# One core, forward and backward of an adaLN block: where the scalings of a gradient's rows run, one product more ahead of a norm gradient's ScalarE steps, and two index operations behind transposed rows

## The chip, the cores and the metric

The kernel runs on one core of one Trainium2 chip. The metric is the device time of one execution in microseconds (us). Below, PE is TensorE, PEld its weight loads, DVE is VectorE, ACT is ScalarE, POOL is GpSimd, SP is SyncE; SPq and ACTq are the instruction queues of SP and ACT, from which they issue DMAs. L548 is line 548 of the kernel before.

## The reference

A forward pass and its vector-Jacobian product. With `mod = silu(c) @ w_mod` cut into six rows of 1024 (sa, ca, ga, sb, cb, gb):

```python
h = layernorm(x) * (1 + ca) + sa
x = x + ga * irfft2(rfft2(h) * (w_r + 1j * w_i))        # S = 2048 tokens, D = 1024
h = layernorm(x) * (1 + cb) + sb
x = x + gb * (gelu(layernorm(h) @ w1 + b1) @ w2 + b2)   # F = 3584
```

The outputs are x and the gradients of A_x, w_r, w_i, w1, b1, w2, b2, c and w_mod for a given `grad_out` of 2048 x 1024. Two of them matter here. The gradient of w_mod is an outer product: for each of the six rows r, `out_9[:, r] = u * gmod[r]`, with u = silu(c) (1024 values) and gmod[r] the gradient of that row of mod (1024 values). The gradient of w1 (`out_4`, 1024 x 3584) is the product of the normalized tokens with the gradient of the MLP's inner layer, summed over 2048 tokens.

## The kernel before, in words

All large products run on PE in bf16 into PSUM tiles of 128 x 512 f32, and everything else is arranged around an order of PE's instructions that is written out by hand. A framework assigns semaphores and buffers, and orders each engine's instructions by priority and by its own estimate of times; `tc.issue_after(x)` ties an instruction to a place behind x on an engine, and `behind(a, b)` makes a follow b in that order without a semaphore. PSUM has three groups of tiles: "s" and "d" with two buffers each, and "f" with four.

**The start.** `grad_out` comes in four blocks of 512 tokens (`gos[0..3]`, loaded by SP from L355, in order with blocks of w_mod, transposed pieces of w2 and the tokens x). `turn_go(j, cch)` (L554) transposes 128 columns of block j: four small products with the identity (L559) into one PSUM tile, from group "s" for even cch and "d" for odd; DVE (even cch, L563) or ACT (odd cch, L566) scales that tile into `gBoT[j]`. The eight turns of block 0 stand alone. The turns of block j+1 are threaded between the 16 products `pp` of block j (L584: two tiles of eight products, each product n reads column block n of `gBoT[j]` and a transposed piece of w2); `TURN_AT` says ahead of which product each turn stands. `pp` takes tiles of group "f", and its results are cast to bf16 on DVE or ACT (L540). Beside this, index tables for the sine and cosine matrices are built: POOL makes products of row and column numbers (L382), and one DVE operation masks them (L413, `trig_idx`). Five of these tables are wanted at the start; the last two go into `gidx2`. Much later (from 57 us) ACT takes sines of them. Behind the start come the remaining products of grad_out with w2 (L548, from 42 us), layer norms of x on DVE and ACT, and folds of the tokens on DVE.

**The last norm gradient.** Near the end the backward inverse transform gives four blocks of tokens; `consume_bwd` (L1580) takes block i through the gradient of the first layer norm: DVE multiplies and sums rows (`scaled_rows`, L1374, giving `s1c`), then four times `ln_bwd` (L1361): one DVE sum (L1365), one ACT operation that needs it and `s1c` (L1368), one DVE addition. To keep PE busy meanwhile, `fill(n)` calls a generator, `pieces()` (L1689), that emits n further pieces of other work. At this place a piece is one tile of out_4: 16 products (L1770, `gw1acc`, a tile of group "f"), a cast on ACT (L1774, `gwo`) and a store. The tuples in `consume_bwd` say how many pieces are emitted at each place. The ACT steps of `ln_bwd` are tied behind the cast of the piece that was emitted last (`w1g["ev"]`).

**The end.** `gw1_quads` (L1654) makes the last two column blocks of out_4 by Strassen-like sums: for each of four column groups c it has seven products of eight matmuls (`gqy`, `gqx`, `gqw`, L1686), ACT copies of intermediate tiles (L1668, `snap`), casts on ACT (L1676) and additions on DVE (L195) that make the results. Through the last pieces, two chains of work on w_mod's gradient run on other engines:

- `gmod_chain` (L1273): for rows 4, 2, 1, 0, eight steps each: load a block of w_mod, multiply and sum with gmod[r] on DVE (L1287, into `gu`). From `gu` come the gradient of c, a small vector (`gc_bf`, L1876), its transpose on PE (L210, `ptr`) and its store.
- `gmod_scaled` (L1293): for the same rows, eight steps each: `gw = gmod[r] * u` for 128 rows of out_9 (128 x 1024 bf16, L1298 on ACT), and its store of 256 KB (L1299, issued by POOL). `gw` goes round five buffers (in the tile `otl`), so scaling n needs the store of scaling n-5 to have landed.

The last loop (L1858) emits, for each of the `left` remaining pieces, the piece, some steps of the chain and one or two steps of the scaling:

```python
        for _ in range(2 if n >= left - 9 else 1):
            next(scaled, None)
```

Of the kernel before, what the change touches and what calls it, by code (L numbers as in the profile page):

```python
# [17 lines left out]
P = 128  # L18
# [17 lines left out]
def kernel(  # L36
# [366 lines left out]
    gslots.update({6 + k: (gidx[:, 1, :], gidx3)[k // 2][:, k % 2 * 512:(k % 2 + 1) * 512] for k in range(4)})  # L403
    trig_in = [None]

    def trig_idx(slot, colv, rowv, nrow, width, modn, cosine):
# [5 lines left out]
        n = nrow * width  # L412
        nc.vector.tensor_scalar(out=idx[:, 0:n], in0=idx[:, 0:n], scalar1=modn - 1, scalar2=None, op0=ALU.bitwise_and)  # L413
        return idx[:, 0:n].rearrange("p (r w) -> p r w", w=width), modn
# [129 lines left out]
    def ph_part(fc, js):  # L544
        for j in js:
# [4 lines left out]
            ph_out(fc, j, pp)  # L550

    turn_in = [None, None]

# [56 lines left out]
    def gen_rows():  # L610
# [7 lines left out]
        return em1  # L618

    def behind(ins, later):  # L620
        tc.add_manual_dep(ins.ins, later.ins.name, mybir.DependencyInfo(mybir.DependencyClass.NoSync, mybir.DependencyReason.DATA),
                          reason="order")

# [669 lines left out]
    def gmod_scaled(rows):  # L1293
        for n in range(len(rows) * NDC):
            k, jc = n // NDC, n % NDC
            gw, r = w1g["gw"][n % 5], rows[k]
            with tc.issue_after(w1g["ev"].ins):
                nc.scalar.activation(out=gw, in_=w1g["gr"][k], func=ACT.Identity, scale=u_rt[:, jc:jc + 1])  # L1298
            nc.gpsimd.dma_start(out=out_9[jc * P:(jc + 1) * P, r * D:(r + 1) * D], in_=gw)  # L1299
            yield  # L1300
# [283 lines left out]
    def consume_bwd(i, o4, tmp, tmp2, n1, eb):  # L1584
# [197 lines left out]
    def fill(n):  # L1782
        for _ in range(n):
            next(todo)
        done[0] += n
# [124 lines left out]
```

## Time and profile before

| | us |
|---|---|
| median of 3 runs | 1373.33 |
| range of these runs | 1371.58 to 1376.87 |
| profiled execution, its own time | 1372.29 |
| span of the profiled execution, first to last instruction | 1370.3 |
| PE busy | 1345.6 (98% of the span) |
| DVE busy | 1077.2 (79%) |
| ACT busy | 792.4 (58%) |
| POOL busy | 390.3 (28%) |

How to read the rows below: a row of the timeline gives the start, the duration and the engine of an instruction (or of xN that follow each other), its line, its operation, out<-in, and in square brackets how long the engine stood idle before it and what ended this. Matmuls are pipelined, so a run of N of them reads a little longer than the distance to the next row. A row of waits gives "engine tile line <- releaser: total us, times, longest us". A row of windows gives the busy us of each engine in a stretch, with the number of instructions, then the granted TensorE clock (1.00 is full), the busy share of the DMA engines and the GB/s.

### The profile page before, as it was taken

The page shows a single profiled execution, that of the slowest core. Times are in us where ns is not written, and L with a number is a line of the kernel's source. Part 1 is how long each engine was busy: PE and PEld are TensorE (multiplying, and loading weights), DVE is VectorE, ACT ScalarE, POOL GpSimd, SP SyncE. Part 2 cuts the span into 40 slices and gives each one's busy share as a digit, 9 for nine tenths or more (in the row PEclk, how much of TensorE's full clock was granted, in tenths as well). Part 3 has the DMA queues.
Part 4 walks back from the last instruction along what each step waited for, and adds up shares of the span by engine and source line. Part 5 has one row for each costly group of instructions (what it writes and reads, how often), then busy time and mean ns, then how long its engine had stood idle before and what let it go on. Part 6 is the DMA issues. An engine that isn't in the chain of part 4 may idle for free. (4 is left out here: it accounts for less than half of the span.)

```text
span 1370.3 us, 18631 instructions
## 1 busy us (share of the span) xinstructions
PE 1345.6 (98%) x6899; PEld 651.0 (48%) x6899; DVE 1077.2 (79%) x1467; ACT 792.4 (58%) x1120; POOL 390.3 (28%) x436
## 2 busy tenths in 40 slices
PE   7999999999999999999999999999999999999997
PEld 4445566444444444444444444444644555444443
DVE  6997889999988878787620578889888488976985
ACT  4864667767877765665414593445732554544456
POOL 6273642411112122212211010112344330332163
PEclk9999999999999999999999999999999999999999
DMA  9975594899787887698999699988579878899876
GB/s 326 322 196 140 160 256 154 250 279 318 262 254 252 212 261 246 199 289 233 284 278 224 181 217 311 296 254 257 179 238 270 222 160 237 207 245 251 201 271 244
DMA packets 356401, 330.08 MB, mean 241 GB/s; under 512 B 203866, under 2 KB 298736, under 8 KB 356182
## 3 DMA queue, kind: packets, MB, share of 16 engines
q1 hardware_dynamic: 314310, 201.02, 57.2%
q0 software_dynamic: 35232, 120.00, 26.0%
q10 hardware_dynamic: 6768, 7.87, 1.7%
q8 instruction: 54, 0.88, 0.3%
q14 instruction: 37, 0.30, 0.1%
HBM read 165.73 MB, written 114.87 MB: 205 GB/s over the span
## 5 line engine op out<-in xcount | busy, mean ns | idle before, releaser
L1230 PE MATMUL pg<-w1T,gzr 128*128 128x512 bf16 x896 | 195.8, 380 | 0.0
L548 PE MATMUL pp<-gBoT,wt 128*128 128x512 bf16 x832 | 185.4, 379 | 3.2 <-ACT pho L540 1.9
L1076 PEld LDWEIGHTS <-w 128*128 128x128 bf16 x896 | 87.2, 98 | 107.4 <-issue 2.9
L1230 PEld LDWEIGHTS <-gzr 128*128 128x128 bf16 x896 | 86.5, 98 | 108.5 <-issue 5.8
L548 PEld LDWEIGHTS <-wt 128*128 128x128 bf16 x832 | 81.0, 98 | 97.9 <-issue 5.3
L1770 PE MATMUL gw1acc<-gzh,n3n 128*128 128x512 bf16 x512 | 111.8, 380 | 0.0
L1076 PE MATMUL pz<-n3Ta,w 128*128 128x512 bf16 x448 | 98.8, 380 | 1.4 <-ACT gt L1079 1.4
L1076 PE MATMUL pz<-n3Tb,w 128*128 128x512 bf16 x448 | 99.0, 380 | 0.0
L1770 PEld LDWEIGHTS <-n3n 128*128 128x128 bf16 x640 | 62.3, 98 | 76.7 <-issue 3.1
L195 DVE TENSOR_TENSOR ct<-ct 128x2048 bf16<-128x2048 bf16 (+1 forms) x84 | 91.5, 1120 | 4.3 <-ACT n L514 2.0
L1079 ACT ACTIVATE gt<-pz,b_col 128x512 bf16<-128x512 f32 x112 | 72.8, 682 | 37.3 <-PE pz L1076 33.1
L1130 PEld LDWEIGHTS <-hhA 128*128 128x128 bf16 x608 | 58.9, 98 | 73.2 <-issue 3.0
L1087 ACT ACTIVATE gt<-gt 128x2048 bf16<-128x2048 bf16 x28 | 53.5, 1911 | 58.3 <-DVE gt L195 58.3
L1411 PE MATMUL gw2acc<-gB,hhsA 128*128 128x512 bf16 x384 | 84.8, 380 | 0.0
L195 DVE TENSOR_TENSOR gt<-gt,gt 128x2048 bf16<-128x2048 bf16 x56 | 68.4, 1223 | 17.7 <-ACT gt L1089 16.8
L1419 ACT CAST gwo<-gw2acc 128x512 bf16<-128x512 f32 x40 | 23.5, 588 | 87.5 <-PE gw2acc L1411 84.2
L1411 PEld LDWEIGHTS <-hhsA 128*128 128x128 bf16 x384 | 37.5, 98 | 43.5
L1083 ACT ACTIVATE gt<-gt 128x2048 bf16<-128x2048 bf16 x28 | 53.4, 1908 | 3.1 <-DVE hhC L195 2.4
L540 ACT CAST pho<-pp 128x512 bf16<-128x512 f32 x68 | 38.6, 584 | 27.3 <-PE pp L548 24.1
L1774 ACT CAST gwo<-gw1acc 128x512 bf16<-128x512 f32 x40 | 23.0, 579 | 53.6 <-PE gw1acc L1770 41.6
L1089 ACT ACTIVATE gt<-gt 128x2048 bf16<-128x2048 bf16 x28 | 53.3, 1905 | 0.3
L1411 PE MATMUL gw2acc<-gB,otl 128*128 128x512 bf16 x224 | 50.0, 380 | 0.0
(414 smaller groups left out, 2710.3 us busy)
## 6 DMA issues: line engine op xcount, KB each, us to landing
gzr<-d_gz SPq DMA_DIRECT2D x28, 512.0 KB
d_ph<-pho POOLq DMA_DIRECT2D x21, 512.0 KB, 5.5
wblk<-in_w_mod_dram SPq DMA_DIRECT2D x10, 1024.0 KB
out_dram<-otl POOLq DMA_DIRECT2D x40, 256.0 KB, 4.1
d_hh<-hhA POOLq DMA_DIRECT2D x19, 512.0 KB, 5.6
wrw<-in_w_mod_dram SPq DMA_DIRECT2D x32, 256.0 KB
w<-in_B_w_dram SPq DMA_DIRECT2D x7, 1024.0 KB
hhC<-d_ph SPq DMA_DIRECT2D x14, 512.0 KB
```

The lines of the kernel that those rows point to most:

```text
L195: return nc.vector.tensor_tensor(out=out, in0=a, in1=b, op=op)
L540: copy(out=ov, in_=pv)
L548: last_pe[0] = nc.tensor.matmul(pp[:], lhsT=wt[:, fc % 4, cch, :], rhs=gBoT[j][:, cch, :], start=(cch == 0), stop=(cch == NDC - 1))
L1076: last_pe[0] = nc.tensor.matmul(pz[:], lhsT=w1s[g][:, cch, k * P:(k + 1) * P], rhs=n3T[:, cch, :], start=(cch == 0), stop=(cch == NDC - 1))
L1079: z_in = nc.scalar.activation(out=zb[:, k, :], in_=pz[:], func=ACT.Identity, bias=b1_col[:, fc:fc + 1], scale=1.0)
L1083: nc.scalar.activation(out=av, in_=zb, func=ACT.Square)
L1087: nc.scalar.activation(out=sg, in_=bv, func=ACT.Sigmoid, scale=2.0 * GK)
L1089: nc.scalar.activation(out=bv, in_=bv, func=ACT.Sigmoid, scale=-2.0 * GK)
L1130: last_pe[0] = nc.tensor.matmul(pbs[i][:], lhsT=hh[:, k, i * P:(i + 1) * P], rhs=wp[:, k, :], start=False, stop=(g == 6 and k == 3))
L1230: last_pg[0] = nc.tensor.matmul(pgs[i][:], lhsT=gzs[b, g][:, k, i * P:(i + 1) * P], rhs=w1Ts[g][:, k, h * KH:(h + 1) * KH], start=(g == 0 ...
L1411: nc.tensor.matmul(acc[:], lhsT=hh_of(fc)[:, t, :], rhs=gBs[t // 4][:, t % 4, h * KH:(h + 1) * KH], start=(t == 0), stop=(t == NT - 1))
L1770: nc.tensor.matmul(acc[:], lhsT=n3ns[t // 4][:, t % 4, cch * P:(cch + 1) * P], rhs=gz2[t // 8][:, t % 8, :], start=(t == 0), stop=(t == NT ...
```

## The change

It has three parts.

1. In the start, the DVE masks of the last two index tables (`idx_in[-2]`, `idx_in[-1]`) are ordered behind the DVE halves of turns 2 and 4 of block 1. `behind` moves up in the file, without a change in it. POOL's part of the tables stays where it is.
2. In `consume_bwd`, block 3 has nine pieces instead of eight ahead of `scaled_rows`, and one instead of two behind it. PE's own order of instructions is the same, word for word.
3. In `gmod_scaled`, rows 4, 2 and 1 are scaled on ACT as before, but their stores are issued by ACT; row 0 is scaled on DVE, with its stores on POOL. The last loop takes two scalings per piece for the first eight pieces, none with the ninth, one per piece for the next eight, and two per piece for the last five (rows 4 and 2, then row 1, then row 0).

```diff
-        nc.vector.tensor_scalar(out=idx[:, 0:n], in0=idx[:, 0:n], scalar1=modn - 1, scalar2=None, op0=ALU.bitwise_and)
+        idx_in.append(nc.vector.tensor_scalar(out=idx[:, 0:n], in0=idx[:, 0:n], scalar1=modn - 1, scalar2=None, op0=ALU.bitwise_and))
...
     first_idx.update({k: token_idx(k) for k in (4, 2, 3)})
+    idx_late = {2: idx_in[-2], 4: idx_in[-1]}
...
                     turn_go(j + 1, TURN_AT.index(n))
+                    if j == 0 and TURN_AT.index(n) in idx_late:
+                        behind(idx_late[TURN_AT.index(n)], turn_in[0])
...
-            with tc.issue_after(w1g["ev"].ins):
-                nc.scalar.activation(out=gw, in_=w1g["gr"][k], func=ACT.Identity, scale=u_rt[:, jc:jc + 1])
-            nc.gpsimd.dma_start(out=out_9[jc * P:(jc + 1) * P, r * D:(r + 1) * D], in_=gw)
+            if k < 3:
+                with tc.issue_after(w1g["ev"].ins):
+                    nc.scalar.activation(out=gw, in_=w1g["gr"][k], func=ACT.Identity, scale=u_rt[:, jc:jc + 1])
+            else:
+                with tc.issue_after(w1g["dve"].ins):
+                    w1g["dve"] = nc.vector.tensor_scalar(out=gw, in0=w1g["gr"][k], scalar1=u_rt[:, jc:jc + 1], scalar2=None,
+                                                         op0=ALU.mult)
+            (nc.scalar if k < 3 else nc.gpsimd).dma_start(out=out_9[jc * P:(jc + 1) * P, r * D:(r + 1) * D], in_=gw)
...
-        fill((0, 6, 6, 8)[i])
+        fill((0, 6, 6, 9)[i])
...
-        fill((4, 1, 2, 2)[i])
+        fill((4, 1, 2, 1)[i])
...
-        for _ in range(2 if n >= left - 9 else 1):
+        for _ in range(2 if n < 8 else 1 if 8 < n < 17 else 2 if n >= left - 5 else 0):
             next(scaled, None)
```

How the order of the instructions changes on DVE and ACT, at the three places that the prediction speaks of. The lines of the changed kernel are a few higher than those of the kernel before (L563 there is L567 here, L1298 is L1302, L1368 is L1376, L1774 is L1782).

DVE at the start, before: `gidx_269` is the tile of the last two index tables, `gBoT_133` and `gBoT_134` are the turned blocks 0 and 1, `gb_col` the column they are scaled with.

```order
L523 COPY gb_col<-pc 128x8
L563 TENSOR_SCALAR gBoT_133,gu<-pt,gb_col 128x512 x4
L413 TENSOR_SCALAR gidx_269<-gidx_269 128x1024
L563 TENSOR_SCALAR gBoT_134,gu<-pt,gb_col 128x512
L413 TENSOR_SCALAR gidx_269<-gidx_269 128x1024
L563 TENSOR_SCALAR gBoT_134,gu<-pt,gb_col 128x512 x3
```

The same place after:

```order
L523 COPY gb_col<-pc 128x8
L567 TENSOR_SCALAR gBoT_133,gu<-pt,gb_col 128x512 x4
L567 TENSOR_SCALAR gBoT_134,gu<-pt,gb_col 128x512 x2
L413 TENSOR_SCALAR gidx_269<-gidx_269 128x1024
L567 TENSOR_SCALAR gBoT_134,gu<-pt,gb_col 128x512
L413 TENSOR_SCALAR gidx_269<-gidx_269 128x1024
L567 TENSOR_SCALAR gBoT_134,gu<-pt,gb_col 128x512
```

The two masks have moved behind the first two turned tiles of block 1. As a consequence of the new order the framework has also re-sorted some casts between DVE and ACT up to about 90 us: ahead of the last mask of a 128 x 512 table in `smax`, DVE has 16 casts from PSUM tiles of 512 columns where it had 19.

ACT from the last norm gradient to the first scalings, before: `ct<-xt,s1c,sc` is the ACT step of `ln_bwd`, `gwo_9683<-gw1acc` the cast of a piece, `otl<-gr,u_rt` a scaling, `accCA` and `accSA` are column sums.

```order
L1774 CAST gwo_9683<-gw1acc 128x512 x7
L1368 ACTIVATE ct<-xt,s1c,sc 128x1024 x3
L1774 CAST gwo_9683<-gw1acc 128x512
L1368 ACTIVATE ct<-xt,s1c,sc 128x1024
L1774 CAST gwo_9683<-gw1acc 128x512
L233 COPY ct<-accCA 64x512
L1774 CAST gwo_9683<-gw1acc 128x512 x2
L1850 ACTIVATE sr<-accSA_10559 1x512
L1850 ACTIVATE sr<-accSA_10560 1x512
L1774 CAST gwo_9683<-gw1acc 128x512
L1298 ACTIVATE otl<-gr,u_rt 128x1024
L1774 CAST gwo_9683<-gw1acc 128x512
```

The same place after:

```order
L1782 CAST gwo_9683<-gw1acc 128x512 x8
L1376 ACTIVATE ct<-xt,s1c,sc 128x1024 x3
L1782 CAST gwo_9683<-gw1acc 128x512
L1376 ACTIVATE ct<-xt,s1c,sc 128x1024
L233 COPY ct<-accCA 64x512
L1782 CAST gwo_9683<-gw1acc 128x512 x2
L1858 ACTIVATE sr<-accSA_10559 1x512
L1858 ACTIVATE sr<-accSA_10560 1x512
L1782 CAST gwo_9683<-gw1acc 128x512
L1302 ACTIVATE otl<-gr,u_rt 128x1024 x2
L1307 DMA out_dram<-otl 128x1024 x2
L1782 CAST gwo_9683<-gw1acc 128x512
```

One cast has moved from behind the fourth `ln_bwd` step to ahead of the first. Two scalings and two DMA issues now stand where one scaling stood.

DVE at the end, before: `wrw,gu<-wrw,gr` is a step of the chain, `t_11132<-gu` and `gc_bf` lead to the gradient of c, `gqx`, `gqy`, `gqw` are the last quarter products.

```order
L195 TENSOR_TENSOR gwo_9683<-gqw,snap 128x512
L1287 ISA wrw,gu<-wrw,gr 128x1024
L1287 ISA gu 128x1
L1287 ISA wrw,gu<-wrw,gr 128x1024
L1287 ISA gu 128x1
L1870 TENSOR_REDUCE t_11132<-gu 128x8
L195 TENSOR_TENSOR t_11132<-t_11132 128x8
L1876 CAST gc_bf<-t_11132 128x8
L195 TENSOR_TENSOR gwo_9683<-gqx,snap 128x512
L195 TENSOR_TENSOR gwo_9683<-gqy,snap 128x512
L211 CAST fin_11127<-ptr 8x128
L195 TENSOR_TENSOR gwo_9683<-gqw,snap 128x512
```

The same place after, from behind the step pair of the chain:

```order
L1305 TENSOR_SCALAR otl<-gr,u_rt 128x1024 x2
L195 TENSOR_TENSOR gwo_9683<-gqx,snap 128x512
L1305 TENSOR_SCALAR otl<-gr,u_rt 128x1024 x3
L1878 TENSOR_REDUCE t_11132<-gu 128x8
L195 TENSOR_TENSOR t_11132<-t_11132 128x8
L1884 CAST gc_bf<-t_11132 128x8
L1305 TENSOR_SCALAR otl<-gr,u_rt 128x1024
L195 TENSOR_TENSOR gwo_9683<-gqy,snap 128x512
L211 CAST fin_11127<-ptr 8x128
L195 TENSOR_TENSOR gwo_9683<-gqw,snap 128x512
```

Six of the eight scalings of row 0 stand in these rows (two more stand ahead of the `gqw` addition of the third column group), five of them ahead of `gc_bf`. On POOL, out of the 32 stores of scalings the last eight are left: two behind its tenth store of quarter products, six behind the eleventh.

More of the change, by code (lines that the diff above doesn't have):

```diff
@@ L403 @@
     gslots.update({6 + k: (gidx[:, 1, :], gidx3)[k // 2][:, k % 2 * 512:(k % 2 + 1) * 512] for k in range(4)})
-    trig_in = [None]
+    trig_in, idx_in = [None], []
     def trig_idx(slot, colv, rowv, nrow, width, modn, cosine):
@@ L550, in ph_part, with behind @@
             ph_out(fc, j, pp)
+    def behind(ins, later):
+        tc.add_manual_dep(ins.ins, later.ins.name, mybir.DependencyInfo(mybir.DependencyClass.NoSync, mybir.DependencyReason.DATA),
+                          reason="order")
     turn_in = [None, None]
@@ L618, in gen_rows @@
         return em1
-    def behind(ins, later):
-        tc.add_manual_dep(ins.ins, later.ins.name, mybir.DependencyInfo(mybir.DependencyClass.NoSync, mybir.DependencyReason.DATA),
-                          reason="order")
     last_pu = [None]
```

## The prediction

> **What bounds the kernel now.** I read the page first, then PE's waits, then the stretches in which PE waits.
>
> ```profile
> span 1370.3 us, 18631 instructions
> PE 1345.6 (98%) x6899; PEld 651.0 (48%) x6899; DVE 1077.2 (79%) x1467; ACT 792.4 (58%) x1120; POOL 390.3 (28%) x436
> ```
>
> PE is busy for 1345.6 of 1370.3 us, in an order that the change leaves alone. So only three things can move the end: the 24.7 us in which PE does nothing, a lower clock, and what follows PE's last product. PE's waits, grouped (total, times, longest), show who owns that idle time:
>
> ```profile
> PE pt L559 <- DVE gBoT L563: 2.6, 2, 2.3
> PE pp L548 <- ACT pho L540: 1.9, 2, 1.7
> PE gw1acc L1770 <- ACT gwo L1774: 1.5, 1, 1.5
> PE pp L548 <- DVE pho L540: 1.2, 2, 0.7
> ...
> PE pt L559 <- DMA fbuf<-in_grad_out_dram: 0.6, 1, 0.6
> ```
>
> The change aims at the first (2.3 us in one wait) and the third (1.5 us); the third part works where no PE wait is seen. Even with both waits gone and nothing late behind them, the kernel would gain a few us of 1370. About 0.5% (6.9 us) is what a measurement of this kernel can tell from no change.
>
> **Part 1, the masks behind the turns.** In the timeline of DVE the mask of a table waits for POOL, and the first turned tile of block 1 waits behind the mask:
>
> ```profile
> 19.33 0.69 DVE L413 TENSOR_SCALAR gidx<-gidx 128x1024 int32<-128x1024 int32 x1 [3.27 <-POOL gidx L382]
> 19.94 0.74 DVE L563 TENSOR_SCALAR_CACHE_REDUCE gBoT<-pt,gb_col 128x512 bf16<-128x512 f32 x1
> ...
> 21.38 0.69 DVE L413 TENSOR_SCALAR gidx<-gidx 128x1024 int32<-128x1024 int32 x1 [0.69 <-POOL gidx L382]
> ```
>
> The tiles of group "s" have two buffers, so PE's fifth turn waits for the first tile to be read. PE's timeline and the windows around it:
>
> ```profile
> 20.74 0.30 PE L559 MATMUL pt<-ident,go 128*128 128x128 bf16 x2 [2.32 <-DVE gBoT L563]
> ...
> 24.03 1.58 PE L584 MATMUL pp<-gBoT,wt 128*128 128x512 bf16 x6
> ...
> 27.64 0.28 PE L559 MATMUL pt<-ident,fbuf 128*128 128x128 bf16 x2
> ...
> 29.40 1.46 PE L584 MATMUL pp<-gBoT,wt 128*128 128x512 bf16 x6
> 31.45 0.28 PE L559 MATMUL pt<-ident,fbuf 128*128 128x128 bf16 x2 [0.60 <-DMA fbuf<-in_grad_out_dram]
> ```
>
> ```profile
> 17.50:20.70 3.20, 0.93 (x9) 0.42 (x6) 1.36 (x3) 1.48 (x5) 2.89 (x5) 1.00 1.03 386
> 20.90:24.20 3.30, 3.30 (x21) 2.14 (x19) 2.81 (x8) 0.78 (x2) 2.70 (x3) 0.50 1.04 385
> 24.30:27.60 3.30, 3.30 (x28) 1.97 (x27) 3.09 (x7) 2.42 (x6) 1.89 (x2) 1.00 1.04 384
> ```
>
> The seventh number from the stretch's length on is the granted clock: after the wait it is 0.50 for some 3.3 us. The price of that: from the fifth turn to the end of six products it takes 24.03 + 1.58 - 20.74 = 4.87 us here, and the same sequence one block later, at full clock, 29.40 + 1.46 - 27.64 = 3.22 us. So the wait costs 2.32 us idle and 1.65 us of slow work, 4.0 us in all.
>
> The Trainium skill ("TensorE: Matmul & The Clock Gate", section "Part 1: The HAM clock gate") says that half rate comes after at least one idle window of about 3.4 us, that such windows run free, and that full rate comes back after a busy one. Read that way, a wait of 2.3 us would cost no clock, and this part could win 2.3 us at most; the row disagrees: PE was busy for 0.93 of 3.20 us, and the clock fell.
>
> What the change does there: DVE reads the first two turned tiles when they are made, then waits for POOL. PE no longer waits at 20.74; it goes on at 18.4 and at full clock. The fourth DVE tile now stands behind the second mask: it can start at 21.38 + 0.61 = 22.0 and ends near 22.75, while PE would want it (as the seventh operand of block 1) near 22.1. I take 0.65 us of new wait. PE would then be ahead by 4.0 - 0.65 = 3.3 us.
>
> But the row at 31.45 says what comes next: block 3 of grad_out is still on its way, and PE waits 0.60 us for it. SP's issues ahead of that load do not wait for PE, and the DMA engines show a busy share of 1.03 to 1.04 in all three windows, so the landing does not move. PE will be there at 27.5 and wait until 31.45, about 4 us. All of the 3.3 us is given back, so part 1 is worth 0 at 31.45.
>
> Then the clock. A wait of 4 us is longer than the one above, so I expect half clock again, from about 31 for 3.4 us; PE works in it from 31.45 on and loses about half of 3 us, 1.5 us. Does that reach the end? Two later waits stand in its way, and DVE is paced by a transfer of its own:
>
> ```profile
> 42.19 0.69 DVE L483 BATCH_NORM_STATS2 st<-x 128x6 f32<-128x512 bf16 x1 [3.19 <-DMA x<-in_A_x_dram]
> ```
>
> ```profile
> 69.83 5.40 PE L548 MATMUL pp<-gBoT,wt 128*128 128x512 bf16 x24 [0.51 <-DVE pho L540]
> ...
> 94.24 1.89 PE L548 MATMUL pp<-gBoT,wt 128*128 128x512 bf16 x8 [1.74 <-ACT pho L540]
> ```
>
> From 42 us on DVE has a backlog that starts with that transfer, not with PE, and PE waits 0.51 and 1.74 us for casts that stand in it. A PE that is 1.5 us later waits 1.5 us less there (2.25 us are to be had). So I take 0 for the clock too. Bounds: if the casts come early, the 1.5 us stay (+1.5); if DVE's three casts fewer in its backlog bring the masks and so the cast of 94.24 forward, up to 0.7 us is won (2.25 - 1.5). Part 1: 0, from -0.7 to +1.5.
>
> **Part 2, one piece ahead of the norm gradient.** ACT and PE there, from their timelines:
>
> ```profile
> 1270.40 0.58 ACT L1774 CAST gwo<-gw1acc 128x512 bf16<-128x512 f32 x1 [2.87 <-PE gw1acc L1770]
> 1282.68 3.52 ACT L1368 ACTIVATE ct<-xt,s1c,sc 128x1024 bf16<-128x1024 bf16 x3 [11.70 <-DVE s1c L1359]
> 1286.11 0.56 ACT L1774 CAST gwo<-gw1acc 128x512 bf16<-128x512 f32 x1
> ```
>
> ```profile
> 1284.62 0.60 PE L215 MATMUL accSA<-otl,ones_bf 128*128 128x512 bf16 x2
> 1286.72 13.54 PE L1770 MATMUL gw1acc<-gzu,n3n 128*128 128x512 bf16 x62 [1.51 <-ACT gwo L1774]
> ```
>
> ACT stands 11.70 us at the first step of `ln_bwd`, with the casts of later pieces behind it. A piece takes PE 16 x 13.54 / 62 = 3.5 us, and group "f" has four tiles: four pieces fill 14 us, and the fifth waits 1.51 us until ACT is through. With one more cast ahead, ACT makes it near 1273.9, inside its 11.70 us of idleness, and PE has a fifth tile: it lasts until about 1285.1 + 3.5 = 1288.6, and the cast at 1286.11 (of the next piece) is over at 1286.7. So the 1.51 us go. What is late next: the third and fourth tile wait for the fourth `ln_bwd` step and the copy of `accCA`, and are free near 1289.5; PE wants them at 1288.6 + 3.5 = 1292. No wait. The clock was not lowered there, so nothing more is won: -1.5. From here to its end PE never waits in this profile, so the gain reaches the end if part 3 takes nothing back. If the gain does not come, 0.
>
> **Part 3, the scalings.** PE's last product and what follows:
>
> ```profile
> 1361.22 1.89 PE L1686 MATMUL gqy<-ct,n3n 128*128 128x512 bf16 x8
> ```
>
> ```profile
> 1363.14 0.58 ACT L1676 CAST gwo<-gqy 128x512 bf16<-128x512 f32 x1 [0.69 <-PE gqy L1686]
> ```
>
> ```profile
> 1363.00:1365.30 2.30, 0.11 (x1) 0.00 (x0) 0.00 (x0) 0.58 (x1) 0.29 (x1) 1.00 0.87 321
> 1365.30:1370.30 5.00, 0.00 (x0) 0.00 (x0) 0.00 (x0) 0.00 (x0) 0.00 (x0) 0.54 0.01 1
> ```
>
> ACT's last cast starts as soon as PE is done: the scalings do not delay it today. Behind it the DMA engines are busy for 1.6 us, and 5 us pass with no work at all. So moving scalings can win only part of that 1.6 us, where the last `gwo` store shares the engines with the last scaled rows; I take 0.2 us, up to 0.6. The scalings themselves, ACT's before and their stores:
>
> ```profile
> 1294.31 1.15 ACT L1298 ACTIVATE otl<-gr,u_rt 128x1024 bf16<-128x1024 bf16 x1
> ...
> 1313.06 1.15 ACT L1298 ACTIVATE otl<-gr,u_rt 128x1024 bf16<-128x1024 bf16 x1 [4.79 <-DMA out_dram<-otl]
> ...
> 1334.06 5.30 ACT L1298 ACTIVATE otl<-gr,u_rt 128x1024 bf16<-128x1024 bf16 x5
> ```
>
> ```profile
> L1299 POOL DMA_DIRECT2D out_dram<-otl x32: 540/540/549, 1310.4 to 1362.7; - x32
> ...
> DMA to landing us min/median/max: 2.2/3.2/7.3
> ```
>
> Five scalings in a row take 5.30 us, 1.06 each. An issue on ACT's queue is not seen for these stores; the nearest rows are ACT's issues of half the size and DVE's scaling of the same size in another stage, whose 256 KB stores took longest to land:
>
> ```profile
> L1421 ACTq DMA_DIRECT2D out_dram<-gwo x25: 338/338/352, 997.4 to 1098.3; - x25
> ```
>
> ```profile
> L1322 DVE TENSOR_SCALAR otl<-otl,u_rt x8: 476/482/486, 1009.4 to 1071.7; 128x1024 bf16<-128x1024 bf16 x8
> ```
>
> ```profile
> DMA to landing us min/median/max: 4.3/7.3/7.9
> ```
>
> Per piece of 3.5 us ACT then has one cast (0.58), two scalings (2.12) and two issues (at most 0.68): 3.4 us. It just keeps up, and group "f" gives it three pieces, 10 us, of slack. The next eight pieces hold one scaling each. DVE's eight scalings are 8 x 0.48 = 3.9 us; seven of them stand ahead of `gc_bf`, for which PE's transpose waits:
>
> ```profile
> 1354.31 0.69 DVE L195 TENSOR_TENSOR gwo<-gqx,snap 128x512 bf16<-128x512 f32 x1 [0.36 <-PE gqx L1686]
> ```
>
> ```profile
> 1359.33 0.22 PE L210 MATMUL ptr<-fin,gc_bf 128*8 128x128 bf16 x1
> ```
>
> After the change the last `gqx` addition can start at 1354.31 - 1.5 = 1352.8 and takes 0.69 us; three scalings of 0.48 us and three small operations on 8 columns follow, so `gc_bf` is there by about 1355.7, and PE wants it at 1359.33 - 1.5 = 1357.8. That leaves 2.1 us, so 0. If a store of that row takes 7.3 instead of 3.2 us to land and the sixth scaling waits for its buffer, the 2.1 us are used up and up to 0.6 us shows.
>
> Part 3: -0.2, from -0.6 to +0.6.
>
> **Sum.** 0 - 1.5 - 0.2 = -1.7 us against the profiled execution: 1372.29 - 1.7 = 1370.6. The median of the three runs is 1.04 us above that execution, so the median comes to 1373.33 - 1.7 = 1371.6. The forecast's own range, from the bounds of parts 1 and 3 without the stay of the clock, is 1370.5 (-0.7 - 1.5 - 0.6 = -2.8) to 1372.4 (0 - 1.5 + 0.6 = -0.9).
>
> **The rivals.**
>
> - *The lower clock lands later and stays.* The half clock moves from 21 to 24 us behind the wait at 31.45, and the two later waits do not absorb it: +1.5 on the sum, 1373.1. For: the clock rows. Against: 2.25 us of waits that hang on DVE. The Trainium skill's page on the clock gate, in the section named above, sides with the half clock: 4 us of idleness hold a whole window of 3.4 us. Chance 0.17.
> - *The block of grad_out is not the limit.* If the load that PE meets at 31.45 lands earlier once PE reads the earlier tiles sooner, part 1 keeps 3.3 us: 1371.6 - 3.3 = 1368.3. Against: the queue's issues don't wait for PE in this stretch. Chance 0.12.
> - *The cast moves and PE waits elsewhere.* If the extra piece only shifts the wait by one tile, part 2 does not do what it says, and the sum is -0.2: 1373.1. Chance 0.08.
> - *ACT is held by its own stores: slower.* A scaling waits for the store five before it. The first 16 scalings go three times round the ring: 3 x (landing + 1.4 us), against eight pieces, 28 us. With 7.9 us, the longest landing above, that is 27.9 us, just enough. Casts stand behind the scalings on ACT, so beyond the 10 us of slack in group "f" PE stands still: it decides from (28 + 10) / 3 - 1.4 = 11.3 us of landing. At 13.5 us PE loses 3 x 2.2 = 6.6 us: 1371.6 + 6.6 = 1378.2. For: the wait of 4.79 us at 1313.06 is this wait, behind a POOL queue that was late. Against: the stores leave POOL's queue. Chance 0.08.
>
> **How the numbers follow.** The forecast has the rest, 0.55. The range takes in the forecast, the first three rivals and the bounds: from 1368.3 - 0.4 = 1367.9 (the second rival with part 3 at -0.6) to 1371.6 + 1.5 + 1.5 + 0.8 = 1375.4 (the first and third together with part 3 at +0.6), put at 1367.5 and 1375.5. Faster by over 0.5% (below 1366.5) would need the second rival and more: 0.03. Slower by over 0.5% (above 1380.2) needs the last rival at its worst: 0.04. Within: 0.93.
>
> **What would show it.** In the profile after: no PE wait for `gBoT` at 20 us, a wait of about 4 us for `fbuf` that ends near 31.4, with granted clock 0.5 behind it; PE at the piece of 94 us within 0.7 us of before. No wait of `gw1acc` for `gwo` near 1285. ACT's waits for `out_dram<-otl` below 5 us in all, no PE wait from 1290 on, and 5 us without work at the end. I am wrong if PE is more than 2 us earlier at 40 us, if a PE wait for ACT or DVE shows up behind 1290, or if POOL or SP finishes last by a us or more.

## The result, and the profile after

The changed kernel takes 1382.43 us (median of 14 runs, 1376.70 to 1389.55), the kernel before 1374.14 us (median of 14 runs on the same chip, 1370.77 to 1382.58). The ratio is 1.0059, with a 95% interval from 1.0038 to 1.0081: slower by 0.6%, where 1371.6 us and no change were forecast. The profiled execution after took 1388.08 us, in the upper part of its runs, and its span is 16.0 us longer than before's; between the medians it is 8.3 us, so the account below is of one long execution.

The page after, first lines:

```profile
span 1386.3 us, 18603 instructions
PE 1347.3 (97%) x6899; PEld 651.8 (47%) x6899; DVE 1078.7 (78%) x1472; ACT 787.2 (57%) x1115; POOL 380.5 (27%) x412
```

PE is busy for 1.7 us more and idle for 14.3 us more. PE's waits after, in the same columns as before's:

```profile
PE gqy L1694 <- ACT snap L1676: 13.1, 1, 13.1
PE pm L283 <- DMA wblk<-in_w_mod_dram: 4.2, 3, 2.4
PE pt L563 <- DMA fbuf<-in_grad_out_dram: 3.9, 2, 2.5
PE pp L548 <- ACT pho L540: 2.8, 4, 2.2
PE accCA L218 <- DVE ct L195: 2.6, 1, 2.6
```

The two waits that the change aims at are gone: `gBoT` at 20 us and `gwo` at 1285 us. In their place stand a wait of 13.1 us that before doesn't have at all, and two smaller ones. PE's timeline at the large one (the third product of the quads waits for the copy of the first):

```profile
1291.03 27.79 PE L1778 MATMUL gw1acc<-gzu,n3n 128*128 128x512 bf16 x128
1318.66 1.89 PE L1694 MATMUL gqy<-gzu,n3n 128*128 128x512 bf16 x8
1320.38 1.89 PE L1694 MATMUL gqx<-gzu,n3n 128*128 128x512 bf16 x8
1335.37 3.57 PE L1694 MATMUL gqy<-gzh,ct 128*128 128x512 bf16 x8 [13.09 <-ACT snap L1676]
1338.73 2.30 PE L1694 MATMUL gqw<-gzh,ct 128*128 128x512 bf16 x8
```

Behind the wait the first two products take 3.57 and 2.30 instead of 1.89 us, another 2.1 us, at a granted clock of 0.50 (up to 1339.6 us). ACT's timeline says why `snap` is late: nothing before it is slow, but ACT stands still twice.

```profile
1311.95 0.59 ACT L1782 CAST gwo<-gw1acc 128x512 bf16<-128x512 f32 x1
1323.33 0.34 ACTq L1307 DMA_DIRECT2D out_dram<-otl  x1
1323.71 2.19 ACT L1302 ACTIVATE otl<-gr,u_rt 128x1024 bf16<-128x1024 bf16 x2 [11.18 <-DMA gr<-d_gmod]
1330.38 0.34 ACTq L1307 DMA_DIRECT2D out_dram<-otl  x1
1330.82 0.59 ACT L1782 CAST gwo<-gw1acc 128x512 bf16<-128x512 f32 x1 [4.92 <-DMA wrw<-in_w_mod_dram]
1334.73 0.59 ACT L1676 COPY snap<-gqy 128x512 f32<-128x512 f32 x1
```

The instruction that waits is not the scaling but the store ahead of it (the `ACTq` row), and what it waits for are transfers of another queue: `gr` and `wrw` are loads of `gmod_chain`, issued by SP. SP's timeline, and POOL's and DVE's from some us earlier:

```profile
1318.05 0.23 SPq L201 DMA_DIRECT2D d_gmod<-row  x1
1319.63 0.33 SPq L1282 DMA_DIRECT2D gr<-d_gmod  x1
```

```profile
1306.36 11.90 POOL L167 DMA_INDIRECT out_dram<-ct,xu  x1 [9.88 <-DVE ct L195]
1318.56 1.48 POOL L167 DMA_INDIRECT out_dram<-ct,xu  x1 [0.30 <-issue]
1320.03 3.81 POOL L1783 DMA_DIRECT2D out_dram<-gwo  x7
```

```profile
1315.08 2.27 DVE L195 TENSOR_TENSOR gzh<-gzh,gzh 128x4096 bf16<-128x4096 bf16 x1
1317.28 0.74 DVE L200 CAST row<-sr 1x512 bf16<-1x512 f32 x2
```

SP stores row 0 of gmod after DVE's casts of it, and loads it back as `gr`. On POOL the first of the two indirect stores of the last block of `out_1` takes 11.90 us; before it took 6.81 us:

```profile
1299.58 6.81 POOL L167 DMA_INDIRECT out_dram<-ct,xu  x1 [10.46 <-DVE ct L195]
```

ACT's second wait hangs on these stores too. DVE's last addition overwrites `ct`, which they read, and waited 4.86 us, until both had landed:

```profile
1324.02 2.29 DVE L195 TENSOR_TENSOR ct<-gzu,gzh 128x4096 bf16<-128x4096 bf16 x1 [4.86 <-issue]
```

The steps of the chain stand behind it on DVE, and SP's loads of `wrw` wait for these steps: SP issues them from 1327.48 us on.

The start and the end. PE meets the products behind the piece of 94 us later (101.14 us before, 103.92 after):

```profile
95.28 3.61 PE L548 MATMUL pp<-gBoT,wt 128*128 128x512 bf16 x16 [2.21 <-ACT pho L540]
98.74 5.34 PE L283 MATMUL pm<-wblk,u_b 128*128 128x512 bf16 x24
```

PE's last product after, and SP's last issue:

```profile
1380.84 1.89 PE L1694 MATMUL gqy<-ct,n3n 128*128 128x512 bf16 x8
```

```profile
1381.76 1.95 SPq L1689 DMA_DIRECT2D out_dram<-gwo  x2
```

PE ends at 1380.84 + 1.89 = 1382.73 us and the program 3.6 us later; before it was 1370.3 - (1361.22 + 1.89) = 7.2 us later. So the 16.0 us are: +2.8 at the start; +1.5 from there to the last pieces (1291.03 instead of 1286.72, 4.3 in all: the 1.5 us at `gwo` are gone, PE waits 2.6 us at `accCA`, and about 0.5 us come in between); +15.3 from the last pieces to PE's last product, `snap` and the slow products behind it; and -3.6 at the end, which the prediction had not foreseen.

### The profile page after: what moved, and what is told of

Read it like the earlier page. It is cut to its first block, busy times and chain, and to the rows that moved or that the text cites. A ratio compares the mean times of both kernels' runs of the same rounds, so it can differ in the third digit from the quotient of the medians.

```text
span 1386.3 us, 18603 instructions
## 1 busy us (share of the span) xinstructions
PE 1347.3 (97%) x6899; PEld 651.8 (47%) x6899; DVE 1078.7 (78%) x1472; ACT 787.2 (57%) x1115; POOL 380.5 (27%) x412
## 5 line engine op out<-in xcount | busy, mean ns | idle before, releaser
L1782 ACT CAST gwo<-gw1acc 128x512 bf16<-128x512 f32 x40 | 23.0, 580 | 55.8 <-PE gw1acc L1778 43.8
```

## The experiments

Each part was run alone first, then each suspect by itself. PE's order is the same in all kernels. The letters in the expectations stand for theories as they were then: A, that ACT is held in the tail, by the semaphores of its stores (A1) or by the ring of five `otl` buffers (A2); D, that the start loses, since the masks hold DVE's casts; E, that the end follows from who issues the last stores; P and P2, that part 1's price is the new place of the casts at the start. The others are told where they stand. The runs:

| kernel | median, us | ratio to before, 95% interval |
|---|---|---|
| mask_only (part 1) | 1375.01 | 1.0030 [1.0015, 1.0044] |
| piece_only (part 2) | 1380.77 | 1.0063 [1.0050, 1.0077] |
| piece_only_again | 1377.64 | 1.0037 [1.0023, 1.0052] |
| scale_only (part 3) | 1377.57 | 1.0040 [1.0025, 1.0054] |
| pool_stores | 1388.38 | 1.0113 [1.0096, 1.0129] |
| dve_order_alone | 1378.55 | 1.0044 [1.0029, 1.0059] |
| piece_dve_as_before | 1373.13 | 0.9999 [0.9981, 1.0017] |
| piece_pair_early | 1372.79 | 1.0014 [0.9995, 1.0033] |
| scale_own_lanes | 1369.71 | 0.9967 [0.9953, 0.9981] |
| last_stores_on_act | 1368.79 | 0.9973 [0.9960, 0.9986] |
| after_both_mended | 1371.94 | 0.9983 [0.9965, 1.0002] |
| mended_without_masks | 1367.76 | 0.9962 [0.9950, 0.9974] |
| all_mended_tie_sine | 1369.72 | 0.9978 [0.9967, 0.9989] |
| masks_tie_sine | 1375.10 | 1.0011 [0.9997, 1.0026] |
| masks_old_casts | 1383.36 | 1.0081 [1.0062, 1.0100] |

**Part by part.** The edits are the hunks of the diff, one part each; `piece_only_again` is the same kernel as `piece_only`, on another chip.

> The kernel before with part 1 alone (the two masks behind turns 2 and 4). Theory A (part 1 is given back at the third block of grad_out; the loss of the whole change is made in the tail by the ACT-issued stores): 0 against the kernel before, within 1 us; PE waits about 4 us for fbuf near 31 us. Theory D (the start loses: PE reaches the products of 101 us 2.8 us later because the masks hold DVE's casts): slower by 2 to 3 us.

> The kernel before with part 2 alone (nine pieces ahead, one behind). Theory A: faster by 1.0 to 1.5 us, the wait of gw1acc for gwo gone, nothing new behind it. If the extra cast disturbs ACT's later steps: 0, with a new PE wait between 1285 and 1300.

> Part 2 alone once more, for a second profile, since the profiled execution of the first was 6 us faster than its median. Theory O: the first indirect store again takes 11.9 us, and PE's wait at the first snap copies is longer than the 2.6 us of the first profile, 5 to 8 us, as ACT's wait for its scaled rows grows with the landing of POOL's stores. If the difference lies elsewhere: a wait of 2 to 3 us there again, and another stretch longer.

> The kernel before with part 3 alone (rows 4, 2, 1 on ACT with stores issued by ACT, row 0 on DVE with stores on POOL, the new counts per piece). Theory A (the whole loss is made here): slower by 6 to 13 us, with a PE wait of several us for an ACT cast or a snap copy between 1295 and 1340, and ACT waiting there behind a store's issue. Theory D: no more than 1 us slower.

Each part alone makes the kernel slower, by 0.3 to 0.6%. In `piece_only` the wait at `gwo` is gone, but a scaling waits for the ring, and `snap` behind it is 2.6 us late for PE in the profile (4.9 us in that of `piece_only_again`, where ACT waits 9.89 us for the ring; before, 4.79 us cost PE nothing):

```profile
1313.61 1.15 ACT L1299 ACTIVATE otl<-gr,u_rt 128x1024 bf16<-128x1024 bf16 x1 [7.63 <-DMA out_dram<-otl]
```

The sum of the three would be 1.1 to 1.3%; together they cost 0.6%. That is less, I take it, because parts 2 and 3 delay the same instruction; no run shows it.

**Part 3: what ACT's stores wait for.** ACT, PE and SP in `scale_only`:

```profile
1301.01 11.82 ACTq L1305 DMA_DIRECT2D out_dram<-otl  x2
1312.87 2.19 ACT L1300 ACTIVATE otl<-gr,u_rt 128x1024 bf16<-128x1024 bf16 x2 [11.30 <-DMA d_gmod<-row]
```

```profile
1323.96 3.50 PE L1692 MATMUL gqy<-gzh,ct 128*128 128x512 bf16 x8 [4.77 <-ACT snap L1674]
```

```profile
1311.30 0.21 SPq L201 DMA_DIRECT2D d_gmod<-row  x1
```

The second store of this pair is issued only at 1301.01 + 11.82 - 0.34 = 1312.49 us, when SP's store of `row` has landed, 1.2 us after the start of that issue. The program's own list of semaphores says why. SP's and ACT's DMAs take eight completion semaphores, DMAHW0 to DMAHW7, in turn; here two users of one of them in program order, with what each waits for:

```
SP  L201  DMA d_gmod <- row     waits DMAHW4, DVE          raises DMAHW4
ACT L1305 DMA out_dram <- otl   waits DMAHW4, Activation   raises DMAHW4
```

ACT's store needs nothing of `row`. It has the same semaphore, so it waits until the transfer before it on that semaphore has landed, and `row` waits for DVE's last small sums. Everything behind it in ACT's order (scalings, casts, `snap`) waits as well. `scale_own_lanes` takes SP out of the turn: the chain's later loads and the store of row 0 go to POOL, whose DMAs have other semaphores.

```diff
+            eng = nc.gpsimd if n >= 14 else nc.sync
-                nc.sync.dma_start(out=w1g["gr"][k], in_=d_gmod[r * D:(r + 1) * D].partition_broadcast(P))
+                eng.dma_start(out=w1g["gr"][k], in_=d_gmod[r * D:(r + 1) * D].partition_broadcast(P))
-            nc.sync.dma_start(out=w1g["wr"][:, n % 4, :], in_=w_mod[jc * P:(jc + 1) * P, r * D:(r + 1) * D])
+            eng.dma_start(out=w1g["wr"][:, n % 4, :], in_=w_mod[jc * P:(jc + 1) * P, r * D:(r + 1) * D])
...
-        nc.sync.dma_start(out=d_gmod[r * D:(r + 1) * D].rearrange("(o n) -> o n", o=1), in_=row[:])
+        (nc.sync if r else nc.gpsimd).dma_start(out=d_gmod[r * D:(r + 1) * D].rearrange("(o n) -> o n", o=1), in_=row[:])
```

> Part 3 alone, with the loads of the last 18 chain steps and the store of the last row of gmod's gradient issued by POOL instead of SP, so that no completion semaphore is shared between SP's DMAs and ACT's stores in the tail. Theory L (ACT's store issues wait for SP's DMAs of the same semaphore): the ACT wait of 11 us for d_gmod is gone, no PE wait for snap or gwo, within 1.5 us of the kernel before. Rival (two scalings per piece are too many for ACT or for the ring): the PE waits of 4.8 and 0.9 us stay, slower by 4 to 6 us.

Measured: no wait of PE in the tail, and part 3 turns from +0.40% to -0.33%. The other way round, `pool_stores` leaves all three parts in and lets POOL issue every store of a scaling:

```diff
-            (nc.scalar if k < 3 else nc.gpsimd).dma_start(out=out_9[jc * P:(jc + 1) * P, r * D:(r + 1) * D], in_=gw)
+            nc.gpsimd.dma_start(out=out_9[jc * P:(jc + 1) * P, r * D:(r + 1) * D], in_=gw)
```

> The changed kernel with one thing undone: the stores of the 24 ACT-scaled tiles are issued by POOL again. Theory A1 (an ACT-issued store waits on ACT's queue for a completion semaphore that it shares with a load of SP, and the casts behind it wait too): the PE wait of 13 us at the snap copies is gone, 1 to 2 us faster than the kernel before. Theory A2 (the ring of five buffers, the prediction's last rival: scalings wait for their stores to land): the wait stays, since ring and number of scalings are the same, slower than before by 5 to 9 us. Theory A3 (two scalings per piece are too much work for ACT): the wait stays too, and no ACT wait for a DMA is seen ahead of it.

It is slower still, by 1.1%, and PE waits 5.7 us for `snap` and 3.1 us for `gwo`. So the semaphores are not the whole cause. ACT now waits for the ring:

```profile
1313.09 1.15 ACT L1302 ACTIVATE otl<-gr,u_rt 128x1024 bf16<-128x1024 bf16 x1 [13.54 <-DMA out_dram<-otl]
```

The stores stand on POOL behind an indirect store of 11.90 us, as in `after`.

**Part 2: why POOL is held.** Part 2 moves one cast and its store, and yet the indirect store takes 6.81 or 6.82 us in before, `mask_only` and `scale_only`, and 11.90 us in `after`, `piece_only`, `piece_only_again` and `pool_stores`, where part 2 is in as it stands. What part 2 also changes is DVE's order at this place, which nobody wrote by hand. The additions from the sum of `accCA` on, before:

```
L195 TENSOR_TENSOR ct<-ct,eb 128x4096
L195 TENSOR_TENSOR rows<-accCA,ct 64x512
L195 TENSOR_TENSOR ct<-ct,n3n 128x2048
L195 TENSOR_TENSOR ct<-n3n,ct 128x2048 x2
L195 TENSOR_TENSOR gzh2<-gzh0,gzu2 128x4096
L195 TENSOR_TENSOR gzh3<-gzh1,gzh2 128x4096
L195 TENSOR_TENSOR sr<-sr 1x512 x2
```

and with part 2:

```
L195 TENSOR_TENSOR rows<-accCA,ct 64x512
L195 TENSOR_TENSOR ct<-ct,eb 128x4096
L195 TENSOR_TENSOR ct<-ct,n3n 128x2048
L195 TENSOR_TENSOR gzh2<-gzh0,gzu2 128x4096
L195 TENSOR_TENSOR ct<-n3n,ct 128x2048
L195 TENSOR_TENSOR sr<-sr 1x512 x2
L195 TENSOR_TENSOR gzh3<-gzh1,gzh2 128x4096
L195 TENSOR_TENSOR sr<-sr 1x512 x2
L195 TENSOR_TENSOR gzh0<-gzh1,gzh0 128x4096
L200 CAST row<-sr 1x512 x2
```

Before, `gzh3` follows `gzh2` and needs its result, and DVE has a gap between them, here of 0.09 us:

```profile
1303.22 2.27 DVE L195 TENSOR_TENSOR gzh<-gzh,gzu 128x4096 bf16<-128x4096 bf16 x1
1305.58 2.29 DVE L195 TENSOR_TENSOR gzh<-gzh,gzh 128x4096 bf16<-128x4096 bf16 x1
```

With part 2 other additions stand in between, and no two of them have a gap until the cast of `row`, which has one input. Three kernels tell order and piece apart, each by a chain of `behind` over these additions: the new order without the piece, the piece with the old order, and the piece with the new order, but `gzh3` directly behind `gzh2`.

```diff
+        seq = [x for k in ["rows", "eb", "S21", "T1", "S40", "sra", "T2", "srb", "B12", "row", "S41", "T4"] for x in dv[k]]
+        for x, y in zip(seq, seq[1:]):
+            behind(y, x)
```

```diff
+        seq = [x for k in ["eb", "rows", "S21", "S40", "S41", "T1", "T2", "sra", "B12", "srb", "T4", "row"] for x in dv[k]]
```

```diff
+        seq = [x for k in ["rows", "eb", "S21", "T1", "T2", "S40", "S41", "sra", "B12", "srb", "row", "T4"] for x in dv[k]]
```

> The kernel before with DVE's last additions tied into the order that they have after the change, and nothing else changed. Theory O: the first indirect store of the last tokens takes 11.9 instead of 6.8 us, ACT waits 7 us or more for a store of scaled rows, PE waits at the first snap copies, slower than before by 5 to 10 us. Theory M: within 1 us of before.

> Part 2 alone, with the last additions of DVE tied into the order that they have in the kernel before (so one ACT cast and its store move, nothing else). Theory O (part 2's loss comes from the order in which DVE now makes its additions: nothing lets POOL's indirect store of the last tokens through, 11.9 us instead of 6.8, and all of POOL's stores, the ring of scaled rows and ACT's casts stand behind it): the store takes 6.8 us again, the PE wait at the first snap copies is gone, 1.0 to 1.5 us faster than the kernel before. Theory M (the moved cast and store themselves disturb ACT and POOL): still slower by 5 to 9 us.

> Part 2 alone, DVE's order as part 2 leaves it, except that the second subtraction of the pair that depend on each other (gzh from gzh and gzh) stands right behind the first, ahead of the others. Theory G (POOL's indirect store gets through only in a gap of DVE, and the pair that wait for each other make one): the first indirect store of the last tokens takes about 3.8 to 4.7 us instead of 11.9 (the span from its start to the pair and 0.8 us more), ACT waits less than 2 us for a store of scaled rows, within 1 us of before or up to 1.5 us faster. If the length of the store goes by the DMA queues: 6.8 or 11.9 us as in the others.

The order alone does it. POOL and PE in `dve_order_alone`, with no piece moved:

```profile
1299.38 11.90 POOL L167 DMA_INDIRECT out_dram<-ct,xu  x1 [10.89 <-DVE ct L195]
```

```profile
1323.03 3.40 PE L1693 MATMUL gqy<-gzh,ct 128*128 128x512 bf16 x8 [4.86 <-ACT snap L1675]
```

With the old order no cost and no gain of the piece is seen (0.9999, and the interval is 2.5 us wide to each side), where 1.0 to 1.5 us were expected. With the pair early the gap comes earlier, and the store ends earlier than it ever did; DVE and POOL in `piece_pair_early`:

```profile
1301.11 2.28 DVE L195 TENSOR_TENSOR gzh<-gzh,gzu 128x4096 bf16<-128x4096 bf16 x1
1303.47 2.29 DVE L195 TENSOR_TENSOR gzh<-gzh,gzh 128x4096 bf16<-128x4096 bf16 x1
```

```profile
1300.33 3.96 POOL L167 DMA_INDIRECT out_dram<-ct,xu  x1 [9.83 <-DVE ct L195]
```

The store ends at 1304.29, 0.90 us after the first addition's end (1301.11 + 2.28 = 1303.39). The same distance holds in `after`: the last addition ahead of the cast of `row` ends at 1315.08 + 2.27 = 1317.35, the store at 1306.36 + 11.90 = 1318.26, 0.91 us later. In all 17 profiles, of every order, it is 0.90 us. With the store short ACT waits 1.4 us for the ring, and the time can't be told from before's (1.0014). So this store's length is the time to the first moment at which DVE runs no addition of two tiles, and 0.9 us.

**The end.** In `scale_own_lanes` PE's last product and SP's last issue:

```profile
1362.77 1.89 PE L1693 MATMUL gqy<-ct,n3n 128*128 128x512 bf16 x8
```

```profile
1363.69 1.95 SPq L1688 DMA_DIRECT2D out_dram<-gwo  x2
```

The span is 1368.0 us, so the program ends 3.3 us behind PE. In every kernel with part 3 it is 3.3 to 3.7 us. POOL's last issue comes before PE's end there, 6.8 to 8.2 us ahead of the end of the program, which lies 2.3 to 2.7 us behind SP's last issue. Where ACT scales all rows and POOL issues all their stores, it is 7.1 to 7.2 us behind PE, and 7.0 us behind POOL's last issue; in before:

```profile
1362.75 0.54 POOL L1299 DMA_DIRECT2D out_dram<-otl  x1 [0.49 <-ACT otl L1298]
```

`last_stores_on_act` takes this alone, from the kernel before:

```diff
-            nc.gpsimd.dma_start(out=out_9[jc * P:(jc + 1) * P, r * D:(r + 1) * D], in_=gw)
+            (nc.scalar if n >= 28 else nc.gpsimd).dma_start(out=out_9[jc * P:(jc + 1) * P, r * D:(r + 1) * D], in_=gw)
```

> The kernel before, with the last four of the 32 scaled stores issued by ACT instead of POOL: same bytes, same order of scalings. Theory E (the program ends some 7 us behind POOL's last issue but only 2.4 us behind SP's or ACT's, so what ends the kernel before is that its last stores stand in POOL's queue): 3 to 4 us faster than before, the end 3.3 to 3.6 us behind PE's last product instead of 7.2. If what counts is how much is still to be stored: no more than 0.5 us faster.

```profile
1363.90 1.89 PE L1686 MATMUL gqy<-ct,n3n 128*128 128x512 bf16 x8
```

```profile
1365.89 0.82 ACTq L1299 DMA_DIRECT2D out_dram<-otl  x2
```

Measured: 0.9973, and 1370.0 - 1365.79 = 4.2 us behind PE's last product instead of 7.2. The missing 0.6 to 0.9 us against the expectation are ACT's last two issues, which end 0.9 us behind PE.

**Part 1.** In `mask_only`, PE and ACT around 94 us:

```profile
94.05 5.30 PE L548 MATMUL pp<-gBoT,wt 128*128 128x512 bf16 x15 [2.21 <-ACT pho L540]
99.18 5.34 PE L283 MATMUL pm<-wblk,u_b 128*128 128x512 bf16 x24
104.36 1.89 PE L548 MATMUL pp<-gBoT,wt 128*128 128x512 bf16 x8
```

```profile
90.86 0.72 ACT L418 ACTIVATE em<-smax,negpi 128x512 bf16<-128x512 int32 x1 [2.20 <-DVE smax L413]
91.61 1.91 ACT L621 ACTIVATE em<-em 128x2048 bf16<-128x2048 bf16 x1
93.43 1.05 ACT L540 CAST pho<-pp 128x512 bf16<-128x512 f32 x2
```

The sine comes at nearly the same time as before (91.05), but two casts stand behind it where before had one. Moving the masks made the framework put 15 of the first 46 casts on the other of ACT and DVE (not 13, as an expectation below has it), and with them ACT's order changed: a cast that is on ACT in both kernels ran at 88.27 us before, ahead of the sine, and runs at 93.43 us here, behind it. So PE has 16 products left behind the wait where before had 8 (the trace has 15 of them), and at a granted clock of 0.50 from 94.5 us on they take 5.13 us (before: 1.73 for the 8). In `after`, at full clock, the same 16 take 3.46 us; with the wait's end at 95.28 instead of 94.24 us that is the 2.8 us at the start. Of these, 2.1 us stand already at the products of 42 us, where nine profiles without part 1 lie 0.0 to 3.8 us behind before's; at the products of 101 us the nine have come to between 0.4 us ahead and 1.9 us behind, and the four with part 1 as it is lie 2.1 to 5.0 us behind. Two kernels tried to take that away. `masks_tie_sine` ties the sine behind the cast that stood ahead of it before (`ph_in` holds the casts); `masks_old_casts` puts all 46 on before's engines.

```diff
+        behind(trig_in[0], ph_in[6, 2])
```

```diff
+            pick()(out=dst, in_=pm[:])
...
+        copy = pick() if fc <= PH_EARLY else nc.vector.tensor_copy if fc >= PH_KEEP and j > 1 else nc.scalar.copy
```

> Part 1 alone, with ACT's last of the four sines at 90 us tied behind the third of the casts that follow, so that no cast of the tiles that PE waits for stands behind it (in the kernel before one did, with part 1 two). Theory P2 (part 1's price is the second cast behind that sine: one tile of 1.7 us less ahead, and half clock behind the longer wait): PE waits less than 1 us for casts between 80 and 100 us, and the time is within 1.5 us of the kernel before. If the price lies elsewhere (later loads, half clock at 25 to 35 us): slower by 2 to 5 us as with the masks alone.

> Part 1 alone, with the first 46 casts of the start's products put by hand on the engines that the framework chose for them in the kernel before (with the masks moved it chooses the other of ACT and DVE for 13 of them). Theory P (part 1's 2 to 3 us come from that choice: one cast more stands behind ACT's sines at 90 us, PE waits for it a tile earlier and falls to half clock): within 1 us of before, PE at the products of 101 us within 1.5 us of before. If the moved masks themselves or the later loads cost: slower by 2 to 4 us as before.

With the tie, PE is at these products at 102.33 instead of 104.36 us, and part 1 costs 0.11% instead of 0.30%, though the two intervals overlap. PE still waits 1.25 us there, now for a cast that the framework has put on DVE. In the second kernel the order at the sine is before's again, with 8 products behind the wait:

```profile
97.89 1.89 PE L554 MATMUL pp<-gBoT,wt 128*128 128x512 bf16 x8 [2.01 <-ACT pho L546]
```

PE is there 3.65 us behind before, but 3.8 us of lateness stand already at 42 us, so in between nothing more is lost. Its time says nothing on the question, since another wait came up in it later (POOL and ACT):

```profile
86.11 29.57 POOL L670 DMA_INDIRECT ws<-in_A_w_i_dram,xu  x1 [0.31 <-issue]
```

```profile
118.95 2.05 ACT L546 CAST pho<-pp 128x512 bf16<-128x512 f32 x4 [13.37 <-DMA d_ph<-pho]
```

DVE is busy for all of these 29.57 us, mostly with additions of two tiles. Its few operations with one input in that stretch did not let this load through, so what was found for the store does not cover it. What else part 1 costs at the start stays open.

**All together.** The three parts with both mendings (DVE's old order, SP out of the turn), then with the tie as well, then parts 2 and 3 with the mendings and without part 1:

> The changed kernel, all three parts, with both mendings: DVE's last additions in the order of before, and the chain's late loads and the store of the last row on POOL. Theories O and L together: no PE wait behind 1290 us; part 1 gives what it gave alone (slower by 2 to 3 us at the start), part 2 wins 1.5 us: between 1 us faster and 2 us slower than before. If a third cause is in the tail: slower by 4 us or more, with a PE wait there.

> The changed kernel with the mendings of the tail (DVE's order of before, the chain's late loads and the last gmod store on POOL) and the same tie of ACT's sine. Theory P2: equal to the mended kernel without part 1 or up to 1 us faster, that is 4 to 6 us faster than before, and so the fastest with all three parts. If the price of part 1 lies elsewhere: 2 to 3 us faster than before, as the mended kernel with all parts.

> The fully mended kernel without part 1: parts 2 and 3, DVE's last additions in their former order, the chain's late loads and the last gmod store on POOL. The step to the mended kernel with all parts is part 1 alone. Theory P (part 1 costs, because it makes the framework choose other engines for the casts of the start): faster than before by 3 to 5 us, 2 to 4 us faster than with part 1. If part 1 is neutral: equal to the mended kernel with all parts, 1 us faster than before.

The last one, 1367.76 us, has the lowest median of all, 0.38% below before; with part 1 it is 0.17% (its interval takes in 1), with the tie 0.22%, 3 us where 4 to 6 were expected. In none of the three does PE wait for ACT in the tail. Most of their gain is at the end of the program, which comes 3.3 to 3.6 us behind PE: `last_stores_on_act` alone has 0.27%, and its interval overlaps that of the fastest.

## Why the prediction was wrong

**Part 1.** Two steps held: the wait for `gBoT` went, and its gain was given back to `fbuf` (waits of 2.51 and 1.37 us there after). The step that failed is "PE at the piece of 94 us within 0.7 us of before": PE is 2.8 us later at the products behind it. The two later waits were taken to hang on a DVE backlog that the change would only shorten. But the re-sorted casts were counted on DVE alone ("three casts fewer"); ACT's order changed with them, and one cast that PE waits for came behind the sine. Nor did "the landing does not move" hold in this execution: PE's second wait for `fbuf` ends at 33.53, not near 31.4 us. The rival of the lower clock did not come in `after`, where the wait was shared out over two blocks. In five other kernels with part 1 the granted clock did fall to 0.50 behind a single wait of 2.19 to 5.24 us for `fbuf`; whether that reaches the end can't be told, since the profiles differ by as much at 42 us without part 1.

**Part 2.** The wait of 1.51 us did go, and the sum's -1.5 was not seen: with the order restored the part measures 0.9999 [0.9981, 1.0017], which holds it (0.9989) as well as nothing. The wait was also partly one execution's own: without part 2 it shows only where DVE waits long for the load of `xt` at 1250 us (9.8 us in before's profile, 9.4 in that of `last_stores_on_act` with a wait of 0.74 us); in the six profiles where DVE waits 3.35 to 5.83 us there is none. The step that failed outright is the silent one, that this part moves one cast and nothing else. It re-orders DVE's last additions, and they hold POOL for 5.1 us more.

**Part 3.** "It just keeps up" was worked out from durations, with an issue at 0.34 us. That duration is right (0.34 us in the single issues of `after` above); what it leaves out is what the issue waits for, and the prediction asked that only of the ring. The rival "ACT is held by its own stores" had the engine, the victims and the sign. Its wait was another: in `scale_only` and `after` ACT is held by transfers of SP, and the ring came in only where POOL issued the stores (13.54 us in `pool_stores`). Its chance of 0.08 was too low, because the case against it ("the stores leave POOL's queue") looked at the queue that they leave and not at the one that they join. This is the step that cost most: 13.1 us of waiting on PE in the profile after, where "no PE wait from 1290 on" was put down.

"So moving scalings can win only part of that 1.6 us" failed in the other direction. The 5 us with no work at all were taken as fixed. They hang on POOL's last issue, which part 3 brings forward, so that SP's last issue decides: part 3 wins 3.6 us at the end where -0.2 was put down.

**The sum.** 0 - 1.5 - 0.2 against medians of +0.30%, +0.37 to 0.63% and +0.40% for the parts alone (about 4, 5 to 9 and 5.5 us), and +0.59% together. "A PE wait for ACT or DVE shows up behind 1290" was named as what would make it wrong, and that is what came.

The Trainium skill ("SBUF — State Buffer", section "Who interferes with whom") says that a DVE instruction with two inputs in SBUF contends with a GpSimd instruction that reads SBUF, through shared ports that only one of them holds at a time. The store that ends 0.9 us behind the first break in such additions agrees, and a rule like it would have warned of part 2. The same section tells of a probe in which `tensor_tensor` did not stall a DMA, and infers the reason; the row of 11.90 us disagrees for this indirect store.

## What to carry to other kernels

After an edit, compare the order of every engine, not of the edited one: where a framework re-plans the rest, a moved cast can cost more through the neighbours than it wins in its place. Before a DMA issue goes to a compute engine's queue, look up what that issue waits for, its semaphore's earlier user among it, and count everything behind it on that engine as waiting too. The last stores of a program are worth a look by themselves: who issues them, and when, set 3 to 4 us here.

## What the runs showed of the hardware

- The first indirect store of the last tokens on POOL took 3.96, 6.81 or 11.90 us, as DVE's additions of two tiles left it a break, and ended 0.90 us behind it. The second store of the pair is not held so (1.48 to 2.06 us under such additions); which step of the first needs the break is open, and so is what ended the indirect load of 29.57 us.
- The end of the program lies 7.0 us behind the last issue of a 256 KB store on POOL, in the nine profiles where that issue ends behind PE's last product, and 3.3 us behind that of the same store on ACT, in the one kernel that has it. Why POOL's take so much longer was not tried.
- After a wait of 13.09 us and after one of 4.77 us, PE's first eight products take 3.57 and 3.50 us instead of 1.89. After one of 2.21 us at the same place the 16 products take 5.13 us in `mask_only` (granted clock 0.50) and 3.46 us in `after` (1.00). Near 25.6 us a wait of 2.19 us for `fbuf` in `mask_only` is followed by a clock of 0.50, one of 3.68 us in `all_mended_tie_sine` by 1.00: the length of a wait alone does not tell whether the clock falls.
